# Scale and offset of the first expert layer: from its output to its activation

## The chip, the core and the metric

One core of a Trainium2 chip runs the whole program. The metric is the device time of one execution in microseconds; a run's time is the median over its executions. The tensor engine (TensorE, PE in the profile) multiplies; VectorE (DVE), ScalarE (ACT) and GpSimd (POOL) work element by element; SyncE (SP) issues transfers. PEld is TensorE's loading of the stationary operand, which runs beside its products.

## The reference

Three layers follow each other, all in float32. The first is a linear attention over 4 batches, 8 heads, 576 positions and 64 features a head: queries and keys pass through a softmax (the keys over the positions, with their maximum over the positions subtracted first), keys times values give a 64 by 64 matrix for each head, and queries times that matrix give 2304 tokens of 512 features. Two layers of 2048 hidden units follow.

```
h = x @ w_in
r = max(h, 0)
g = s * (r * r) + b          # s and b are one number each
x = g @ w_out                # first layer
h = x @ w_in2
g = h * tanh(softplus(h))
out = g @ w_out2             # second layer
```

The weights come as 64-bit floats, which the kernel turns into float32 on chip.

## The kernel before

**Steps.** The tokens are cut into five chunks of 512, 256, 512, 512 and 512. A step is one chunk with one block of 128 of the 2048 hidden units: 16 steps a chunk, 80 for the first layer (`ph` 0), then 80 for the second (`ph` 1). In a step `emit_h` makes h of a block from x, the activation makes g, and `emit_y` adds g times the block of `w_out` into the chunk's y, which stays in PSUM for 16 steps and is copied out by `y_out`. h is made two steps (`LEAD`) ahead of the y that uses it, in the second layer three.

**High and low halves.** Most products are made in three passes over a rounded high half and a low half: `split` lets ScalarE copy a tile to its high half (L171) and VectorE subtract it for the low half (L168, `minus`); `passes` issues three matmuls (L178). A step has 24 of them, 12 for h and 12 for y. The first steps of chunk 0 use whole float32 weights instead (L231, L284).

**The first layer's activation.** `emit_relu2` lets ScalarE take Relu out of PSUM (L258) and Square in place (L259), then splits. So g lacks s and b. `y_out` multiplies by s as it copies y out of PSUM (L313 on VectorE, L319 on ScalarE). The offset b reaches y as b times the column sums of `w_out`: `colsum` lets GpSimd add up the 32 blocks of `w_out`, high and low (L554, L556), into `acc`; `colsum_mm` sums over the partitions with eight narrow matmuls (L562) and multiplies by b (L566) into `bsum`; `x_split` adds `bsum` where the second layer takes its input (L202, L203).

**Attention.** A chunk's attention runs during the chunk before it, for two heads at a time (`hp` 0 to 3), in stages `att1` to `att5` one or two steps apart. Where a chunk reaches into a new batch, the keys are loaded into one buffer `kb` (L346, L350), and `att1` finds their maxima: a reduction on VectorE (L405), a transpose on TensorE (L410), a second reduction (L411), a product with the identity (L412), and a product with a tile of ones that spreads the maxima over all partitions (L413). `att2` subtracts them from the keys (L428), and with that frees `kb`. For the queries, L418 and L419 subtract maxima, L441 to L443 form reciprocal sums, L451 scales. L496 to L502 finish the 64 by 64 matrices, L471, L480 and L178 with `x` are TensorE's part.

**Weights.** `conv_bits` and `conv_split` turn 64-bit weights into float32 halves, five instructions on VectorE and a split for each of 16 pieces a layer; the first layer's in the first 140 us, the second layer's from the last chunk of the first layer on.

**Order.** `todo` and `run` put the stages at steps. That fixes the order in which the program is written; a planner with costs of its own then orders the instructions of each engine and sets buffers and semaphores. Each engine runs its list strictly in order, and SyncE its transfers, each of which waits for its buffer.

Of the kernel before, what the change touches and what calls it, by code (L numbers as in the profile page):

```python
# [26 lines left out]
def kernel(  # L27
# [47 lines left out]
    sb_s = const.tile([P, 1], F32, name="sb_s")  # L75
    sb_b = const.tile([P, 1], F32, name="sb_b")
    ones = const.tile([P, P], F32, name="ones")
    bsum = const.tile([P, NK], F32, name="bsum")
    y_dram = [dram.tile([P, NK, CHUNKS[c]], F32, name=f"yd{c}") for c in range(NC)]


# [88 lines left out]
    def split(hi, lo, src, eng=None):  # L170
        nc.scalar.copy(out=hi, in_=src)  # L171
        minus(eng or nc.vector, lo, src, hi)
# [21 lines left out]
    def x_split(ph, c, kk):  # L194
        n = CHUNKS[c]
        src = x_next.pop((ph, c, kk))
        hi, lo = (t[:, 0:n] for t in x_tiles(kk, f"{ph}_{c}_{kk}"))
        if ph == 0:
            split(hi, lo, src)
        else:  # L200
            b = bsum[:, kk:kk + 1]
            nc.scalar.activation(out=hi, in_=src, func=AF.Identity, bias=b)  # L202
            nc.vector.scalar_tensor_tensor(  # L203
                out=lo, in0=src, scalar=b, in1=hi.bitcast(F32), op0=ALU.add, op1=ALU.subtract
            )
        x_t[ph, c, kk] = (hi, lo)

    def x2_load(c):
# [40 lines left out]
    def emit_relu2(m):  # L249

        c = steps[m][1]
        if whole_y(m):
            r = gp.tile([P, CM], F32, tag="gl", name=f"r{m}")[:, 0:CHUNKS[c]]
            g_t[m] = (None, r)
        else:
            r = rp.tile([P, CM], F32, tag="r", name=f"r{m}")[:, 0:CHUNKS[c]]
            hi, lo = g_tiles(m)
        nc.scalar.activation(out=r, in_=h_ps.pop(m), func=AF.Relu)  # L258
        nc.scalar.activation(out=r, in_=r, func=AF.Square)  # L259
        if not whole_y(m):  # L260
            split(hi, lo, r)

    def emit_mish(m):

# [27 lines left out]
    def y_out(n):  # L292
        ph, c, _ = steps[n]
        nt = CHUNKS[c]
        nm = NK if ph == 0 else nt // P
        w = nt if ph == 0 else DM
        if ph == 0:
            to = y_dram[c]
        else:
            to = out[T0[c]:T0[c] + nt, :].rearrange("(p r) d -> p r d", p=P)  # L300
        for m, ps in enumerate(y_ps.pop((ph, c))):
            if m % 2 == 0:
                pair = cv.tile([P, 2 * DM], F32, tag="t", name=f"ys{m}_{n}")
                pair = pair.rearrange("p (i d) -> p i d", i=2)
            ys = pair[:, m % 2, 0:w]
            if n == 2 * NS - 1 and m == nm - 1:
                nc.sync.dma_start(out=to[:, m - 1, :], in_=pair[:, 0, 0:w])
                for copy, o in ((nc.scalar.copy, slice(0, w // 2)), (nc.vector.tensor_copy, slice(w // 2, w))):
                    copy(out=ys[:, o], in_=ps[:, o])
                    nc.sync.dma_start(out=to[:, m, o], in_=ys[:, o])  # L310
                continue
            if m % 2 and ph == 0:
                nc.vector.tensor_scalar(  # L313
                    out=ys, in0=ps[:, 0:w], scalar1=sb_s, scalar2=None, op0=ALU.mult
                )
            elif m % 2:
                nc.vector.tensor_copy(out=ys, in_=ps[:, 0:w])
            elif ph == 0:
                nc.scalar.activation(out=ys, in_=ps[:, 0:w], func=AF.Copy, scale=sb_s)  # L319
            else:  # L320
                nc.scalar.copy(out=ys, in_=ps[:, 0:w])
            if m % 2:
                nc.sync.dma_start(out=to[:, m - 1:m + 1, :], in_=pair[:, :, 0:w])
# [66 lines left out]
    def att1(b, c, hp):  # L390

        if b is not None:
            kb = kv_in[b, hp][0]
            if b == 0:
                ke = q_raw[hp][:, 2 * DM:4 * DM]
                km = ke[:, RK * P:(RK + 1) * P]
                kc = ke[:, (RK + 1) * P:(RK + 1) * P + 1]
                ke = ke[:, 0:RK * P].rearrange("p (r h d) -> p r h d", r=RK, h=2)
            else:
                ke = ap.tile([P, RK, 2, D], F32, tag="ke", name=f"ke{b}_{hp}")  # L400
                km = ap.tile([P, P], F32, tag="km", name=f"km{b}_{hp}")
                kc = ap.tile([P, 1], F32, tag="kc", name=f"kc{b}_{hp}")


            nc.vector.tensor_reduce(  # L405
                out=km.rearrange("p (h d o) -> p h d o", h=2, o=1),
                in_=kb.rearrange("p h r d -> p h d r"), axis=AX.X, op=ALU.max,
            )
            ps = att_ps(b == 0, hp % 2, f"km{b}_{hp}")
            nc.tensor.transpose(ps[:, 0:P], km, ident)  # L410
            nc.vector.tensor_reduce(out=kc, in_=ps[:, 0:P], axis=AX.X, op=ALU.max)  # L411
            nc.vector.tensor_scalar(out=km, in0=ident, scalar1=kc, scalar2=None, op0=ALU.mult)  # L412
            nc.tensor.matmul(out=ps[:, P:2 * P], lhsT=ones, rhs=km, start=True, stop=True)  # L413
            kv_mid[b, hp] = (ps[:, P:2 * P].rearrange("p (h d) -> p h d", h=2), ke)
        rq = CHUNKS[c] // P
        t = q_in[c, hp].rearrange("p h r d -> p (h r) d")
        mx = ap.tile([P, 2 * CM // P, 1], F32, tag="qm", name=f"qm{c}_{hp}")[:, 0:2 * rq, :]
        nc.vector.tensor_reduce(out=mx, in_=t, axis=AX.X, op=ALU.max)  # L418
        (nc.vector if c else nc.gpsimd).tensor_tensor(  # L419
            out=t, in0=t, in1=mx.to_broadcast([P, 2 * rq, D]), op=ALU.subtract  # L420
        )

    def att2(b, c, hp):
        if b is not None:
            kb = kv_in[b, hp][0]
            km, ke = kv_mid[b, hp]
            for h in range(2):
                nc.vector.tensor_tensor(  # L428
                    out=ke[:, :, h, :], in0=kb[:, h], in1=km[:, h:h + 1, :].to_broadcast([P, RK, D]),
                    op=ALU.subtract,  # L430
                )
        nc.scalar.activation(out=q_in[c, hp], in_=q_in[c, hp], func=AF.Exp)

    def att3(b, c, hp):
        if b is not None:
            ke = kv_mid[b, hp][1]
            nc.scalar.activation(out=ke, in_=ke, func=AF.Exp)
        rq = CHUNKS[c] // P
        t = q_in[c, hp].rearrange("p h r d -> p (h r) d")
# [22 lines left out]
    def att4_mm(b, c, hp):  # L462

        if b is not None:
            vb = kv_in.pop((b, hp))[1]
            ke = kv_mid.pop((b, hp))[1]
            ps = att_ps(b == 0, hp % 2, f"kv{b}_{hp}")
            kv_ps[b, hp] = ps
            for r in range(RK):
                for h in range(2):  # L470
                    nc.tensor.matmul(  # L471
                        out=ps[h * D:(h + 1) * D, 0:D + 1], lhsT=ke[:, r, h],
                        rhs=vb[:, r, h * (D + 1):(h + 1) * (D + 1)],
                        start=(r == 0), stop=(r == RK - 1),
                    )
# [67 lines left out]
        x_next[0, c, hp] = t  # L543


    acc = []

    def colsum(f):
        if f == 0:
            acc.append(wp.tile([P, 4 * DM], F32, tag=f"w{WHOLE - 1}", name="acc")[:, 0:DM])  # L550
        for i, w in enumerate(W[0, "wo", f]):
            w = w.bitcast(F32)
            if f == 0 and i == 0:
                op = nc.gpsimd.tensor_copy(out=acc[0], in_=w)  # L554
            else:
                op = nc.gpsimd.tensor_tensor(out=acc[0], in0=acc[0], in1=w, op=ALU.add)  # L556
            tc.keep_in_program_order(op)

    def colsum_mm():
        ps = ps_a.tile([P, CM], F32, tag="a", name="bsum_ps")  # L560
        for kk in range(NK):
            nc.tensor.matmul(  # L562
                out=ps[:, kk:kk + 1], lhsT=acc[0][:, kk * P:(kk + 1) * P], rhs=ones[:, 0:1],
                start=True, stop=True,
            )
        nc.vector.tensor_scalar(  # L566
            out=bsum, in0=ps[:, 0:NK], scalar1=sb_b, scalar2=None, op0=ALU.mult
        )


    todo = {}

    def at(slot, what, fn, *args):
# [29 lines left out]
            at(s + o[4], "att5_mm", att5_mm, b, c, hp)  # L603
    for i, c in enumerate(ORDER2):
        at((NC - 1 + i) * NF, "load", x2_load, c)
    for f in range(NF):
        at(2 * NF + 12 + f, "sum", colsum, f)
    at(3 * NF + 12, "sum", colsum_mm)

# [18 lines left out]
    for hp in range(NP):  # L630
# [4 lines left out]
        if hp:  # L635
            v_load(0, hp - 1)
    v_load(0, NP - 1)
    run(-3, "load")
    bds.append(ap.tile([P, P], F32, name="bd"))
    nc.vector.memset(bds[NP], 0.0)  # L640
    v_pads(vb1)
    nc.gpsimd.memset(kb1[REST:P, :, RK - 1, :], -3.0e38)
    nc.sync.dma_start(out=sb_s, in_=moe_s[0:1].partition_broadcast(P))
    nc.sync.dma_start(out=sb_b, in_=moe_b[0:1].partition_broadcast(P))
    run(-2, "load")
    for hp in range(NP):
        for stage in (att1, att2, att3, att4_mm, att4, att5, att5_mm):
# [8 lines left out]
    for n in range(2 * NS):  # L656
# [12 lines left out]
        for m in hs:  # L669
# [6 lines left out]
                emit_relu2(m)  # L676
                continue
            emit_mish(m)
        run(n, "att5_mm", "att4", "att1", "sum")
        if not boundary and n < 2 * NS - 2:  # L680
            emit_y(n)
        elif n == 2 * NS - 2:
# [43 lines left out]
```

## Time and profile before

| | |
|---|---|
| median of 3 runs | 896.02 us (896.01 to 896.61) |
| profiled execution, its own time | 897.58 us |
| its span, first to last instruction | 895.8 us |
| TensorE busy | 861.5 us, 96% |
| VectorE / ScalarE / GpSimd busy | 415.2 / 349.6 / 54.4 us |
| mean granted TensorE clock | 0.988 |

All views are of the one profiled execution. Its time is longer than its span by what lies before the first and behind the last instruction. An engine that is busy all the time need not be at its peak: the granted clock says at which of its two levels, 1.2 or 2.4 GHz, TensorE ran. In the timeline, square brackets hold the idle time in front of an instruction and what ended it.

### The profile page before, as it was taken

Reading aid. Unit: us, or ns where it says so; the run is one execution under the profiler, and the core shown is the slowest. Engines: PE = TensorE matmul, PEld = TensorE weight load, DVE = VectorE, ACT = ScalarE, POOL = GpSimd, SP = SyncE. Lnnn points to the kernel's source line nnn. Section 1 sums busy time; section 2 is a strip of 40 time slices with the busy share of each in tenths; the row PEclk is TensorE's granted clock in tenths of the full one; section 3 lists DMA queues with packets and bytes.
Section 4 is the critical chain, followed back from the end, with each engine's and each line's share of the span. In section 5 each row is a group of like instructions: output and inputs, shape, how many; then the busy total and the mean of one; then the engine's idle time right before and its main releaser. Section 6 shows DMA issues by size and latency. Waiting matters only on the chain.

```text
span 895.8 us, 10587 instructions
## 1 busy us (share of the span) xinstructions
PE 861.5 (96%) x4220; PEld 698.8 (78%) x4220; DVE 415.2 (46%) x667; ACT 349.6 (39%) x627; POOL 54.4 (6%) x65
## 2 busy tenths in 40 slices
PE   4799997879999999999999999999999999999997
PEld 3344786879888888888888888888889888888886
DVE  6989988866354422225883488311112211121111
ACT  3645674435554543444545233321122321132211
POOL 4000006920000000000000000000000000000000
PEclk9999997989999999999999999999999999999999
DMA  8992114122111010022542152010011100001001
GB/s 226 314 369 66 33 30 120 27 56 59 50 42 47 12 48 12 1 83 105 188 142 78 63 182 101 25 48 0 1 48 48 45 27 1 0 1 48 1 0 48
DMA packets 59490, 62.56 MB, mean 70 GB/s; under 512 B 24240, under 2 KB 51120, under 8 KB 59440
## 3 DMA queue, kind: packets, MB, share of 16 engines
q1 hardware_dynamic: 58352, 60.83, 21.2%
q10 hardware_dynamic: 1088, 1.05, 0.4%
q8 instruction: 33, 0.54, 0.3%
q14 instruction: 17, 0.14, 0.0%
HBM read 52.43 MB, written 9.44 MB: 69 GB/s over the span
## 4 chain that ended last, share of the span: by engine, by line
PE 91%; DVE 4%; DMA 2%; SPq 1%; issue 1%; ACT 0%; POOL 0%; DVEq 0%
PE y L178 41%; PE h L178 40%; PE h L231 4%; PE y L284 3%; DMA kb<-in_k_dram 2%; PE x L178 1%; PE kv L471 1%; PE qt L480 1%; DVE qn L451 1%; DVE gl L168 1%; DMA kvb<-in_k_dram 1%; PE km L413 0%; DVE km L412 0%; DMA q<-in_q_dram 0%; DVE qs L442 0%
## 5 line engine op out<-in xcount | busy, mean ns | idle before, releaser
L178 PE MATMUL h<-xh,w 128*128 128x512 f32 (+1 forms) x1208 | 367.3, 371 | 0.0
L168 DVE TENSOR_TENSOR gl<-r,gh 128x512 fp32r<-128x512 f32 (+1 forms) x152 | 100.7, 664 | 343.5 <-ACT r L269 259.2
L178 PEld LDWEIGHTS h<-xh,w 128*128 128x128 f32 x1208 | 223.7, 191 | 38.3 <-ACT r L258 0.3
L178 PE MATMUL h<-xl,w 128*128 128x512 f32 (+1 forms) x604 | 223.4, 370 | 0.7 <-DVE xl L168 0.7
L178 PE MATMUL y<-gh,w 128*128 128x512 f32 (+1 forms) x584 | 178.3, 370 | 0.0
L178 PE MATMUL y<-w,gh 128*128 128x512 f32 x568 | 175.1, 390 | 0.0
L268 ACT ACTIVATE gh<-h 128x512 fp32r<-128x512 f32 (+1 forms) x79 | 43.8, 555 | 242.0 <-PE y L178 216.8
L178 PEld LDWEIGHTS h<-xl,w 128*128 128x128 f32 x604 | 115.5, 191 | 19.9 <-DVE xl L168 0.9
L178 PEld LDWEIGHTS y<-w,gh 128*128 128x128 f32 x568 | 105.6, 188 | 21.1
L178 PEld LDWEIGHTS y<-gh,w 128*128 128x128 f32 x584 | 107.7, 190 | 17.7
L178 PE MATMUL y<-gl,w 128*128 128x512 f32 (+1 forms) x292 | 108.4, 372 | 2.9 <-DVE gl L168 2.8
L178 PE MATMUL y<-w,gl 128*128 128x512 f32 x284 | 110.3, 389 | 0.0
L258 ACT ACTIVATE r<-h 128x512 f32<-128x512 f32 (+1 forms) x80 | 44.1, 554 | 111.9 <-PE h L178 103.5
L178 PEld LDWEIGHTS y<-gl,w 128*128 128x128 f32 x292 | 55.6, 190 | 12.2 <-DVE gl L168 3.4
L178 PEld LDWEIGHTS y<-w,gl 128*128 128x128 f32 x284 | 53.3, 188 | 11.2
L171 ACT CAST w<-t 128x1024 fp32r<-128x1024 f32 x32 | 33.5, 1051 | 53.6 <-DVE t L154 50.1
L259 ACT ACTIVATE r<-r 128x512 f32<-128x512 f32 (+1 forms) x80 | 46.8, 589 | 1.8
L269 ACT ACTIVATE r<-h 128x512 f32<-128x512 f32 (+1 forms) x80 | 44.0, 551 | 0.0
L171 ACT CAST gh<-r 128x512 fp32r<-128x512 f32 (+1 forms) x73 | 41.7, 574 | 3.2 <-PE y L178 1.5
L556 POOL TENSOR_TENSOR acc<-acc,w 128x512 f32<-128x512 f32 x31 | 41.8, 1349 | 2.4
L168 DVE TENSOR_TENSOR w<-t,w 128x1024 fp32r<-128x1024 f32 x32 | 39.0, 1220 | 4.0 <-ACT w L171 3.9
L150 DVE SCALAR_TENSOR_TENSOR t<-raw,t 128x1024 int32<-128x1024 int32 x32 | 39.0, 1222 | 0.2
(102 smaller groups left out, 605.3 us busy)
## 6 DMA issues: line engine op xcount, KB each, us to landing
raw<-in_moe_w_in_dram SPq DMA_DIRECT2D x32, 512.0 KB, 5.3
raw<-in_moe_w_out_dram SPq DMA_DIRECT2D x32, 512.0 KB, 6.8
yd<-ys SPq DMA_DIRECT2D x8, 512.0 KB, 2.6
x<-yd SPq DMA_DIRECT2D x16, 256.0 KB, 3.8
out_dram<-ys SPq DMA_DIRECT2D x8, 512.0 KB, 2.7
kb<-in_k_dram SPq DMA_DIRECT2D x12, 256.0 KB, 2.9
vb<-in_v_dram SPq DMA_DIRECT2D x24, 128.0 KB, 3.0
kvb<-in_k_dram SPq DMA_DIRECT2D x4, 256.0 KB, 3.7
```

What stands on the lines that cost most here:

```text
L150: nc.vector.scalar_tensor_tensor(out=ti, in0=high, scalar=-0x40000000, in1=ti, op0=ALU.bitwise_and, op1=ALU.bitwise_or,)
L168: eng.tensor_tensor(out=lo, in0=src, in1=hi.bitcast(F32), op=ALU.subtract)
L171: nc.scalar.copy(out=hi, in_=src)
L178: mm = nc.tensor.matmul(out=ps, lhsT=x, rhs=y, start=start, stop=stop)
L231: nc.tensor.matmul(out=h_ps[m], lhsT=wl[:, o], rhs=x_whole[kk], start=kk == 0, stop=kk == NK - 1,)
L258: nc.scalar.activation(out=r, in_=h_ps.pop(m), func=AF.Relu)
L259: nc.scalar.activation(out=r, in_=r, func=AF.Square)
L268: nc.scalar.activation(out=hi, in_=h_ps[m], func=AF.Mish)
L269: nc.scalar.activation(out=r, in_=h_ps.pop(m), func=AF.Mish)
L284: nc.tensor.matmul(out=ps[:, 0:nt], lhsT=wl[:, o], rhs=gl, start=f == 0, stop=False)
L451: (nc.vector if c else nc.gpsimd).tensor_tensor(out=qn[:, :, h, :], in0=t[:, o, :], in1=sm[:, o, :].to_broadcast([P, rq, D]), op=ALU.mult)
L556: op = nc.gpsimd.tensor_tensor(out=acc[0], in0=acc[0], in1=w, op=ALU.add)
```

## The change

g is made as the reference has it. In chunks 0 and 1 ScalarE applies s and b after Square with one more instruction. In chunks 2 to 4 VectorE makes s r r from r, ScalarE adds b as it makes the high half, and VectorE adds b and subtracts the high half for the low one. `colsum`, `colsum_mm`, `acc` and `bsum` go; `y_out` copies without s, and `x_split` splits the second layer's input as it does the first's. s and b are loaded ahead of the first weights. Besides, the product that spreads the key maxima (L413) moves from the end of `att1` to the head of `att2`, one step later.

```
-    bsum = const.tile([P, NK], F32, name="bsum")
...
-        if ph == 0:
-            split(hi, lo, src)
-        else:
-            b = bsum[:, kk:kk + 1]
-            nc.scalar.activation(out=hi, in_=src, func=AF.Identity, bias=b)
-            nc.vector.scalar_tensor_tensor(
-                out=lo, in0=src, scalar=b, in1=hi.bitcast(F32), op0=ALU.add, op1=ALU.subtract
-            )
+        split(hi, lo, src)
...
         nc.scalar.activation(out=r, in_=h_ps.pop(m), func=AF.Relu)
-        nc.scalar.activation(out=r, in_=r, func=AF.Square)
-        if not whole_y(m):
-            split(hi, lo, r)
+        if c < 2:
+            nc.scalar.activation(out=r, in_=r, func=AF.Square)
+            nc.scalar.activation(out=r, in_=r, func=AF.Identity, scale=sb_s, bias=sb_b)
+            if not whole_y(m):
+                split(hi, lo, r)
+            return
+        nc.vector.scalar_tensor_tensor(
+            out=r, in0=r, scalar=sb_s, in1=r, op0=ALU.mult, op1=ALU.mult
+        )
+        nc.scalar.activation(out=hi, in_=r, func=AF.Identity, bias=sb_b)
+        nc.vector.scalar_tensor_tensor(
+            out=lo, in0=r, scalar=sb_b, in1=hi.bitcast(F32), op0=ALU.add, op1=ALU.subtract
+        )
...
-            if m % 2 and ph == 0:
-                nc.vector.tensor_scalar(
-                    out=ys, in0=ps[:, 0:w], scalar1=sb_s, scalar2=None, op0=ALU.mult
-                )
-            elif m % 2:
+            if m % 2:
                 nc.vector.tensor_copy(out=ys, in_=ps[:, 0:w])
-            elif ph == 0:
-                nc.scalar.activation(out=ys, in_=ps[:, 0:w], func=AF.Copy, scale=sb_s)
             else:
                 nc.scalar.copy(out=ys, in_=ps[:, 0:w])
...
             nc.vector.tensor_scalar(out=km, in0=ident, scalar1=kc, scalar2=None, op0=ALU.mult)
-            nc.tensor.matmul(out=ps[:, P:2 * P], lhsT=ones, rhs=km, start=True, stop=True)
-            kv_mid[b, hp] = (ps[:, P:2 * P].rearrange("p (h d) -> p h d", h=2), ke)
+            kv_mid[b, hp] = (ps[:, P:2 * P], km, ke)
...
     def att2(b, c, hp):
         if b is not None:
             kb = kv_in[b, hp][0]
-            km, ke = kv_mid[b, hp]
+            ps, km, ke = kv_mid[b, hp]
+            nc.tensor.matmul(out=ps, lhsT=ones, rhs=km, start=True, stop=True)
+            km = ps.rearrange("p (h d) -> p h d", h=2)
...
-    acc = []
-
-    def colsum(f):
...
-    def colsum_mm():
...
-    for f in range(NF):
-        at(2 * NF + 12 + f, "sum", colsum, f)
-    at(3 * NF + 12, "sum", colsum_mm)
...
     v_load(0, NP - 1)
+    nc.sync.dma_start(out=sb_s, in_=moe_s[0:1].partition_broadcast(P))
+    nc.sync.dma_start(out=sb_b, in_=moe_b[0:1].partition_broadcast(P))
     run(-3, "load")
...
-    nc.sync.dma_start(out=sb_s, in_=moe_s[0:1].partition_broadcast(P))
-    nc.sync.dma_start(out=sb_b, in_=moe_b[0:1].partition_broadcast(P))
     run(-2, "load")
```

## Rows read from the trace of the kernel before

**Rows 1.** The page's 40 equal slices: busy share in tenths, TensorE and GpSimd.

```profile
PE   4799997879999999999999999999999999999997
...
POOL 4000006920000000000000000000000000000000
```

**Rows 2.** Windows, 143 to 191.6 us: stretch, length, busy (instructions) by engine, granted clock, DMA.

```profile
core 0: us, PE busy (x) PEld busy (x) DVE busy (x) ACT busy (x) POOL busy (x), PEclk, DMA share, GB/s
142.97:151.22 8.25, 2.84 (x17) 1.99 (x16) 7.61 (x14) 2.19 (x7) 7.78 (x7) 0.77 0.61 179
151.22:157.60 6.38, 6.33 (x28) 6.04 (x29) 3.71 (x7) 3.01 (x8) 6.07 (x5) 0.50 0.25 83
157.60:181.18 23.58, 20.71 (x191) 19.54 (x190) 20.62 (x24) 9.95 (x25) 22.25 (x18) 1.00 0.10 27
...
185.73:191.60 5.87, 5.87 (x27) 5.87 (x28) 2.18 (x8) 3.35 (x8) 0.00 (x0) 0.50 0.18 50
```

**Rows 3.** TensorE's timeline, its three longest gaps behind 45 us.

```profile
151.22 0.80 PE L413 MATMUL km<-km,ones 128*128 128x128 f32 x2 [3.72 <-DVE km L412]
...
161.76 0.39 PE L178 MATMUL y<-gl,w 128*128 128x256 f32 x1 [1.96 <-DVE gl L168]
...
185.73 0.80 PE L413 MATMUL km<-km,ones 128*128 128x128 f32 x2 [4.55 <-DVE km L412]
```

**Rows 4.** GpSimd's timeline, 128 to 200 us.

```profile
141.41 44.19 POOL L556 TENSOR_TENSOR acc<-acc,w 128x512 f32<-128x512 f32 x31
```

**Rows 5.** VectorE's groups by form, 140.7 to 185.6 us: count, busy us, mean ns, idle before.

```profile
L168 DVE TENSOR_TENSOR gl<-r,gh 128x256 fp32r<-128x256 f32 x8 | 7.8, 1000 | 0.0
L451 DVE TENSOR_TENSOR qn<-q,qs 128x256 f32<-128x256 f32 x4 | 5.7, 1452 | 0.0
L412 DVE TENSOR_SCALAR km<-ident,kc 128x128 f32<-128x128 f32 x3 | 3.8, 1257 | 0.0
L442 DVE TENSOR_SCALAR qs<-qs 128x8 f32<-128x8 f32 x3 | 3.7, 1239 | 0.0
...
L405 DVE TENSOR_REDUCE km<-kb 128x128 f32<-128x640 f32 x2 | 2.6, 1324 | 4.4 <-DMA kb<-in_k_dram 4.4
```

**Rows 6.** VectorE's groups by form, 190 to 260 us.

```profile
L405 DVE TENSOR_REDUCE km<-kb 128x128 f32<-128x640 f32 x4 | 5.2, 1312 | 2.5 <-DMA kb<-in_k_dram 2.5
...
L451 DVE TENSOR_TENSOR qn<-q,qs 128x256 f32<-128x256 f32 x8 | 3.0, 422 | 5.3 <-PE x L178 5.3
L168 DVE TENSOR_TENSOR gl<-r,gh 128x256 fp32r<-128x256 f32 x7 | 2.9, 415 | 3.3 <-ACT gh L171 3.3
...
L412 DVE TENSOR_SCALAR km<-ident,kc 128x128 f32<-128x128 f32 x3 | 0.9, 286 | 0.1
...
L442 DVE TENSOR_SCALAR qs<-qs 128x8 f32<-128x8 f32 x4 | 0.7, 167 | 0.0
```

**Rows 7.** Windows, 84 to 140 us.

```profile
84.00:140.00 56.00, 56.00 (x282) 43.63 (x281) 50.05 (x83) 39.37 (x64) 0.00 (x0) 1.00 0.15 39
```

**Rows 8.** ScalarE's groups by form from 190, VectorE's from 260, to 860 us.

```profile
L259 ACT ACTIVATE r<-r 128x512 f32<-128x512 f32 x48 | 30.3, 632 | 1.1
...
L202 ACT ACTIVATE xh<-x,bsum 128x512 fp32r<-128x512 f32 x16 | 10.8, 722 | 1.5 <-PE h L178 1.5
...
L203 DVE SCALAR_TENSOR_TENSOR xl<-x,bsum,xh 128x512 fp32r<-128x512 f32 x16 | 11.1, 749 | 2.1 <-ACT xh L202 2.1
```

**Rows 9.** TensorE's timeline at 396 us.

```profile
396.01 0.95 PE L562 MATMUL bsum_ps<-ones,acc 128*128 128x1 f32 x8
```

**Rows 10.** Windows, two stretches of chunk 4.

```profile
419.68:430.56 10.88, 10.88 (x50) 9.01 (x49) 9.98 (x13) 5.33 (x8) 0.00 (x0) 1.00 0.31 103
474.08:484.96 10.88, 10.88 (x50) 9.01 (x49) 1.70 (x3) 3.93 (x8) 0.00 (x0) 1.00 0.16 65
```

**Rows 11.** Timelines of SyncE's queue and of ScalarE at the start.

```profile
19.77 0.43 SPq L643 DMA_DIRECT2D sb_s<-in_moe_s_dram  x1
...
23.94 1.15 ACT L142 ACTIVATE t<-raw 128x1024 f32<-128x1024 f32 x1
```

**Rows 12.** The chain that ended last, at 153 us: start, us, what.

```profile
153.40 3.80 DMA kb<-in_k_dram
```

More of the change, by code (lines that the diff above doesn't have):

```diff
@@ L435, in att3 @@
         if b is not None:
-            ke = kv_mid[b, hp][1]
+            ke = kv_mid[b, hp][2]
             nc.scalar.activation(out=ke, in_=ke, func=AF.Exp)
@@ L465, in att4_mm @@
             vb = kv_in.pop((b, hp))[1]
-            ke = kv_mid.pop((b, hp))[1]
+            ke = kv_mid.pop((b, hp))[2]
             ps = att_ps(b == 0, hp % 2, f"kv{b}_{hp}")
@@ L543, in att5_mm @@
         x_next[0, c, hp] = t
-    acc = []
-    def colsum(f):
[L549 to L557, printed above, removed]
-    def colsum_mm():
[L560 to L568, printed above, removed]
     todo = {}
@@ L678 @@
             emit_mish(m)
-        run(n, "att5_mm", "att4", "att1", "sum")
+        run(n, "att5_mm", "att4", "att1")
         if not boundary and n < 2 * NS - 2:
```

## The prediction

> **What bounds the kernel now.** I began with the page's forty slices [rows 1]. TensorE stands at 9 tenths nearly everywhere, so only its gaps can be won, and they lie in two places: the first two slices, and slices 7 to 9, where it reads 7, 8 and 7. GpSimd's row reads 6, 9 and 2 in exactly those three slices and nothing after. A slice is 895.8 / 40 = 22.4 us, so the place is 134 to 201 us: the end of chunk 0 and most of chunk 1, the narrow one.
>
> Next I cut this place at the gaps with the view of windows [rows 2]. TensorE's idle time is length less busy time: 8.25 - 2.84 = 5.41 us, 6.38 - 6.33 = 0.05 and 23.58 - 20.71 = 2.87; between the third row's end and the fourth's begin lies one more gap, the 4.55 us of [rows 3]. Together 12.88 us. Two rows, 6.38 and 5.87 us long, show a granted clock of 0.50, which is 1.2 instead of 2.4 GHz, each right behind a gap of about 4 us. Before the third, 1.96 us gap of [rows 3] the clock was 1.00, and in its window it stayed 1.00.
>
> Then TensorE's timeline says what ended the gaps [rows 3]: both long ones end at L413, the product that spreads the key maxima, waiting for VectorE's L412; the third waits for the low half of g. All three are VectorE's lateness. Why it is late shows in its own groups by form, once inside GpSimd's stretch [rows 5] and once behind it [rows 6]; GpSimd's stretch is one row, 31 additions in 44.19 us [rows 4], 1.4 us each. Same line, same shape, two prices: the low half of g 1000 against 415 ns, L451 1452 against 422, L442 1239 against 167 although it touches only 8 columns, L412 1257 against 286. The control is L405, a reduction with one input: 1324 against 1312. So some VectorE instructions sit out a GpSimd addition and others don't. The four groups lose 8 x 0.585 + 4 x 1.030 + 3 x 1.072 + 3 x 0.971 = 14.9 us, more than TensorE's whole idle time here.
>
> This is what the Trainium skill's page "SBUF — State Buffer", section "Who interferes with whom", states: VectorE and GpSimd share one pair of ports, taken for a whole instruction, by VectorE instructions with two inputs in SBUF or in a two-port mode, and never by a reduction. The groups agree (1239 against 167, 1324 against 1312); a reader who trusts the rows alone gets the same sum.
>
> **The change, part by part.**
>
> *GpSimd's column sums go.* VectorE gets its 14.9 us back, and the gaps that its lateness made should close. How far? In the first window (5.41 us idle) the delayed work ahead of TensorE is one L442, one pair of L451 and one L412: 1.07 + 2.06 + 0.97 = 4.10 us, which leaves 1.31. That is plausible, since there TensorE needs the last part of x for chunk 1 and has little else to do. Bounds: 0 to 5.41; I take 1.31. Ahead of the 4.55 us gap are one each of L442 and L412, a pair of L451 and a low half: 1.07 + 0.97 + 2.06 + 0.59 = 4.69, so nothing is left. For the 2.87 us between them, the 1.96 of [rows 3] among them, 14.9 - 4.10 - 4.69 = 6.1 us of lateness are left; I take 0. Idle time won: 12.88 - 1.31 = **11.6 us** (bounds 4.6, if 5.41 and 2.87 stay, and 12.9).
>
> *The clock.* With gaps of at most 1.3 us the clock should stay up, as it did around the 1.96 us gap. Work of 6.33 and 5.87 us at half the clock [rows 2] then takes half: 3.17 + 2.94 = **6.1 us** won. Bounds: 0, if a gap like the 3.72 us one stays, to 6.1.
>
> *The eight small products of the sums* [rows 9] sit among dense TensorE work: **0.95 us** won (0 at least).
>
> *The product moved to the next step.* It issues no DMA, and the count stays. In [rows 3] it is where TensorE stood twice; a step later, L412 has the y products' time to finish, so the move is a second cover for the same gaps, not a second gain. What it costs: the subtraction from the keys (L428) follows it, the reload of the single key buffer follows that, and on VectorE the row sums of the step queue behind the subtraction. The spreading itself is 0.8 us of TensorE on either side of the move. Where the kernel had no gap I take 0, for TensorE has y and h products on both sides to run; the price without that cover is the first rival's.
>
> *g = s r^2 + b in chunks 0 and 1* adds one ScalarE instruction a step. The trace of before has none with scale and bias from a tile in this place; the nearest are Square at 632 ns and the biased copy L202 at 722 [rows 8]. Sixteen in chunk 0 are 10.1 to 11.6 us, off TensorE's path as long as ScalarE keeps up. From 84 to 140 us, the fullest part, it is busy 39.37 of 56.00 us [rows 7]; about ten steps fall into it, 7.2 us, and 9.4 stay free. TensorE is busy all 56.00 us there, and h runs two steps ahead of y. One step is 24 products, 5.2 us by the 50 in 10.88 us of [rows 10], so 0.7 us more of latency is covered: 0. Without cover it would be 11.6 us.
>
> *In chunks 2 to 4* (48 steps) ScalarE loses its Square and VectorE gains a product of 749 ns by L203's form [rows 8]; the chain to g now passes from ScalarE to VectorE and back twice. The fullest row of VectorE is 9.98 of 10.88 us at 420 us, while second-phase weights are converted [rows 10]. Two more instructions make 11.48: over by 0.6. But the conversions are what fills it and they can slip: at 474 us VectorE is busy 1.70 of 10.88. Taken: 0; the price if not is the last rival's.
>
> *Evictions and second-phase input* only lose an operand. *Loads of s and b* move ahead of the first weight loads on SyncE's queue, which then start 2 x 0.43 = 0.86 us later [rows 11]. ScalarE's first use of weights, at 23.94 us, begins right behind its previous instruction, so part of this is hidden; VectorE is the bound of that stretch. Bounds 0 and 0.86; I take **+0.3**.
>
> **Sum** against the profiled execution: 897.58 - 11.6 - 6.1 - 0.95 + 0.3 = 879.2. The median of the runs is 896.02, 1.56 below that execution, so 877.7.
>
> **The rivals.**
>
> *The key loads take the gaps over.* There is one key buffer; its reload needs the subtraction, and the subtraction now waits for the later product. The chain shows one such load at 3.80 us [rows 12], and VectorE stood 4.4 us for two inside GpSimd's stretch [rows 5]. For it: behind that stretch VectorE still waits 2.5 us for four [rows 6]. Against it: TensorE is not held there. If two loads come to lie on the path, 7.6 us return, and with one gap long enough a half-clock stretch of 3.2: 885 to 888.5.
>
> *The lateness isn't GpSimd's.* Then only the small products go: 897.58 - 0.95 + 0.3 - 1.56 = 895.4, no measurable change. Against it stands the split between two-input work and reductions.
>
> *Slower: the longer chain to g starves y in chunks 2 to 4.* If VectorE's queue, over-full at 420 us, makes TensorE wait at each of the 48 steps, the gain of 18.3 us is eaten at 0.38 us a step; at 0.5 it is 24 us and 902. For it: 11.48 us of work for 10.88. Against it: h leads by two steps, 10 us, against some 3 us of chain, and the fullness is work that can be put off.
>
> **How the numbers follow.** My forecast has a chance of 0.62, the key loads 0.22, the unrelated lateness 0.06, the starved y 0.06, and 0.04 is for mixtures that keep some of the gain. All won, the floor is 897.58 - 12.9 - 6.1 - 0.95 - 1.56 = 876.1. The forecast's own range is 875.8 to 882; the upper end of mine, 887.5, takes in two thirds of the key-load case and leaves 0.19 out. A measurement of this kernel tells some 0.2%, 1.8 us, from no change. Faster by more: 0.62 + 0.22 + 0.04 = 0.88; within: 0.06, the second rival; slower: 0.06, the third.
>
> **What would show it.** Right: GpSimd empty after 30 us; L442 near 170 and L451 near 420 ns in chunk 1; no wait above 2 us at L413; the granted clock at 1.00 from 140 to 200 us; TensorE dense from 45 us to the tail but for a gap of about 1.3 us at the start of chunk 1. Wrong: a TensorE wait for keys or q (first rival), the old prices of L442 without GpSimd (second), or waits of y for the low half of g in chunks 2 to 4 (third). My weakest step is the 1.31 us left over at the chunk's start: the instruction order is planned anew, and work that I count as hidden may land on that path.

## The result, and the profile after

The changed kernel takes **881.5 us** (median of 4 runs, 880.89 to 881.83) beside 896.01 (4 runs, 895.22 to 896.61): the ratio is 0.9838, 95% interval [0.9821, 0.9855]. Run again in a later group it took 883.36 (5 runs, 881.35 to 884.3) beside 896.47, ratio 0.9851 [0.9836, 0.9866]. The forecast of 877.7 lies below all these runs; its range holds them.

Page slices of the changed kernel, TensorE, GpSimd and granted clock, to be laid beside [rows 1]:

```profile
PE   4799998999999999999999999999999999999997
...
POOL 4000000000000000000000000000000000000000
PEclk9999999999999999999999999999999999999999
```

GpSimd is empty behind the first slice, and where TensorE read 7, 8, 7 it reads 8, 9, 9. The reason is in VectorE's groups by form, 139 to 205 us, which answer to [rows 5] (the names of lines have moved: L439 was L442, L448 was L451, L408 was L412, L401 was L405, and, for later, L406 was L410, L425 was L428 and L422 is the moved L413):

```profile
L167 DVE TENSOR_TENSOR gl<-r,gh 128x256 fp32r<-128x256 f32 x16 | 6.7, 421 | 5.5 <-ACT gh L170 5.5
L401 DVE TENSOR_REDUCE km<-kb 128x128 f32<-128x640 f32 x4 | 5.2, 1298 | 5.1 <-DMA kb<-in_k_dram 5.1
L448 DVE TENSOR_TENSOR qn<-q,qs 128x256 f32<-128x256 f32 x10 | 3.8, 421 | 3.0 <-PE x L177 2.9
...
L408 DVE TENSOR_SCALAR km<-ident,kc 128x128 f32<-128x128 f32 x5 | 1.4, 277 | 0.0
L439 DVE TENSOR_SCALAR qs<-qs 128x8 f32<-128x8 f32 x6 | 1.0, 165 | 0.0
```

The four disturbed groups fell to the prices of [rows 6]; the one-input reduction L401 stayed at 1298 ns. What TensorE still waits for, from 44 us to the tail (wait, total us, times, longest):

```profile
PE km L406 <- DVE km L401: 1.3, 1, 1.3
PE km L422 <- DVE km L408: 0.8, 1, 0.8
PE h L177 <- DVE xl L167: 0.3, 1, 0.3
PE h L177 <- ACT r L250: 0.2, 1, 0.2
```

All four lie between 140 and 155 us. The two long waits for the spreading product [rows 3] are gone, but a new one heads the list: the key transpose L406, waiting for the key maximum L401. And between the end of chunk 0 and the tail the clock still falls once (windows of 1 us in the changed kernel):

```profile
145.00:146.00 1.00, 0.48 (x4) 0.48 (x4) 0.89 (x3) 0.50 (x2) 0.00 (x0) 1.00 1.01 210
146.00:147.00 1.00, 0.78 (x7) 0.58 (x5) 0.88 (x2) 0.41 (x2) 0.00 (x0) 0.99 0.78 228
147.00:148.00 1.00, 0.98 (x4) 0.98 (x5) 0.42 (x1) 1.00 (x3) 0.00 (x0) 0.50 0.63 211
...
149.00:150.00 1.00, 1.00 (x7) 1.00 (x7) 0.69 (x1) 0.97 (x2) 0.00 (x0) 0.50 0.35 96
150.00:151.00 1.00, 1.00 (x9) 1.00 (x8) 0.00 (x0) 1.00 (x4) 0.00 (x0) 0.80 0.06 13
```

From 147 to 150 us TensorE is busy at a granted clock of 0.50, that is 1.2 GHz.

**One table for all traces.** Every trace is cut at two points of TensorE's timeline: the end of chunk 0's last y product, and the first y product of chunk 2. Between them, *idle* is length less busy time, and *clock* is busy time times (1 less granted clock), summed over windows of 1 us. *Rest* is what remains of the span, dense work in the main. Microseconds:

| kernel | chunk 0 ends | idle | clock | rest | span |
|---|---|---|---|---|---|
| before | 141.60 | 12.87 | 6.31 | 735.02 | 895.8 |
| changed | 140.56 | 2.65 | 1.64 | 734.25 | 879.1 |
| changed, later group (e12) | 141.54 | 3.82 | 1.69 | 734.25 | 881.3 |
| e1, no sums | 141.57 | 3.78 | 1.69 | 733.66 | 880.7 |
| e2, move only | 141.46 | 11.49 | 6.38 | 734.57 | 893.9 |
| e3, not moved | 141.58 | 2.58 | 1.63 | 734.51 | 880.3 |
| e4, sums back | 140.52 | 12.19 | 6.31 | 734.98 | 894.0 |
| e5, sums late | 141.63 | 3.82 | 1.56 | 735.59 | 882.6 |
| e6, loads back | 140.54 | 4.72 | 3.39 | 734.35 | 883.0 |
| e7, no reload | 140.84 | 1.33 | 0.00 | 735.23 | 877.4 |
| e8, pair earlier | 142.55 | 3.34 | 0.00 | 734.91 | 880.8 |
| e9, all VectorE | 140.86 | 6.87 | 4.39 | 735.48 | 887.6 |
| e10, all ScalarE | 141.99 | 2.84 | 1.65 | 734.22 | 880.7 |
| e11, pair later | 141.01 | 4.28 | 1.70 | 736.31 | 883.3 |

The rest stays within 1.4 us of before's; nearly the whole effect is idle and clock time in this one place. For the changed kernel the terms against before are -1.04, -10.22, -4.67 and -0.77, together -16.7; in the later group -0.06, -9.05, -4.62 and -0.77, together -14.5. These are differences of single traced executions; by medians the changed kernel is 14.5 us faster in the first group (896.01 - 881.5) and 13.1 in the later one (896.47 - 883.36).

### The profile page after: what moved, and what is told of

It is laid out like the page before. It is cut to its first block, busy times and chain, and to the rows that moved or that the text cites. A ratio compares the mean times of both kernels' runs of the same rounds, so it can differ in the third digit from the quotient of the medians.

```text
span 879.1 us, 10563 instructions
## 1 busy us (share of the span) xinstructions
PE 854.4 (97%) x4212; PEld 693.2 (79%) x4212; DVE 431.0 (49%) x714; ACT 344.2 (39%) x611; POOL 12.4 (1%) x33
## 4 chain that ended last, share of the span: by engine, by line
PE 95%; DVE 2%; DMA 1%; ACT 1%; issue 0%; POOL 0%; SPq 0%; DVEq 0%; ACTq 0%
PE y L177 43%; PE h L177 42%; PE h L223 4%; PE y L286 3%; PE x L177 1%; PE kv L468 1%; PE qt L477 1%; DMA kvb<-in_k_dram 1%; DMA kb<-in_k_dram 0%; PE km L422 0%; DVE q L401 0%; PE x L525 0%; DVE xl L167 0%; PE km L406 0%; DVE qs L438 0%
## 5 line engine op out<-in xcount | busy, mean ns | idle before, releaser
L167 DVE TENSOR_TENSOR gl<-r,gh 128x512 fp32r<-128x512 f32 (+1 forms) x104 | 63.1, 608 | 265.3 <-ACT r L271 259.6
L177 PE MATMUL y<-gl,w 128*128 128x512 f32 (+1 forms) x292 | 106.6, 367 | 0.0
L257 DVE SCALAR_TENSOR_TENSOR r<-r,sb_s 128x512 f32<-128x512 f32 x48 | 35.9, 748 | 56.4 <-ACT r L250 56.3
L260 ACT ACTIVATE gh<-r,sb_b 128x512 fp32r<-128x512 f32 x48 | 34.8, 724 | 37.6 <-DVE r L257 34.9
L261 DVE SCALAR_TENSOR_TENSOR gl<-r,sb_b,gh 128x512 fp32r<-128x512 f32 x48 | 35.9, 749 | 21.0 <-ACT gh L260 20.8
```

What stands on the lines that cost most here:

```text
L167: eng.tensor_tensor(out=lo, in0=src, in1=hi.bitcast(F32), op=ALU.subtract)
L177: mm = nc.tensor.matmul(out=ps, lhsT=x, rhs=y, start=start, stop=stop)
L257: nc.vector.scalar_tensor_tensor(out=r, in0=r, scalar=sb_s, in1=r, op0=ALU.mult, op1=ALU.mult)
L260: nc.scalar.activation(out=hi, in_=r, func=AF.Identity, bias=sb_b)
L261: nc.vector.scalar_tensor_tensor(out=lo, in0=r, scalar=sb_b, in1=hi.bitcast(F32), op0=ALU.add, op1=ALU.subtract)
```

## The experiments

The theory is that of the prediction: GpSimd's additions hold up VectorE in chunk 1, TensorE waits for VectorE, its clock falls. The rivals are the moved product (that the gain comes from the move), the key load, and the new forms of g.

| run | median us (range, runs) | before, same group | ratio, 95% interval |
|---|---|---|---|
| e1 | 882.17 (881.45 to 883.95, 4) | 895.93 | 0.985 [0.9829, 0.9871] |
| e2 | 895.09 (893.91 to 896.53, 10) | 895.93 | 0.9995 [0.9983, 1.0006] |
| e3 | 882.94 (882.07 to 884.51, 4) | 895.93 | 0.9861 [0.9837, 0.9885] |
| e4 | 896.1 (894.23 to 896.92, 10) | 895.93 | 1.0003 [0.9993, 1.0013] |
| e5 | 884.62 (882.0 to 885.15, 4) | 895.86 | 0.9873 [0.9854, 0.9892] |
| e6 | 885.27 (882.62 to 886.19, 4) | 895.86 | 0.9881 [0.9861, 0.9902] |
| e7 | 880.01 (879.13 to 880.46, 4) | 895.86 | 0.9829 [0.9812, 0.9845] |
| e8 | 882.1 (880.39 to 882.62, 4) | 895.86 | 0.9847 [0.9831, 0.9863] |
| e9 | 889.64 (889.38 to 891.83, 4) | 896.47 | 0.9928 [0.9914, 0.9942] |
| e10 | 882.61 (881.92 to 883.1, 4) | 896.47 | 0.9843 [0.983, 0.9857] |
| e11 | 885.24 (884.09 to 886.54, 4) | 896.47 | 0.9874 [0.986, 0.9887] |
| e12 | 883.36 (881.35 to 884.3, 5) | 896.47 | 0.9851 [0.9836, 0.9866] |

**e1: before, without the column sums** (and so without b).

```
-    for f in range(NF):
-        at(2 * NF + 12 + f, "sum", colsum, f)
-    at(3 * NF + 12, "sum", colsum_mm)
...
+    nc.vector.memset(bsum, 0.0)
```

Expected: 

> The kernel before without the column sums on GpSimd and without their eight small products; the offset that they carry is set to zero, so b is left out of the result. Nothing else is changed. If VectorE's lateness from 141 to 186 us is GpSimd's doing, L442 falls from 1239 to about 170 ns and L451 from 1452 to about 420 there, and the time falls by most of what the change won: 881 to 885 us. If the moved product or the new form of g made the gain, the old prices stay and the time is 894 to 896 us.

Measured: 882.17 us, about the whole gain with one part of the change. VectorE's prices fell as expected: L442 to 166 and L451 to 421 ns from 139 to 205 us.

**e2: before, with the spreading product moved, alone.**

```
-            nc.tensor.matmul(out=ps[:, P:2 * P], lhsT=ones, rhs=km, start=True, stop=True)
...
     def att2(b, c, hp):
...
+            nc.tensor.matmul(out=ps, lhsT=ones, rhs=km, start=True, stop=True)
```

Expected: 

> The kernel before with the spreading product alone moved from the end of att1 to the head of att2. If the gaps are VectorE's lateness, the product only meets it elsewhere: L442 stays near 1240 ns, and 892 to 897 us come out. If TensorE's place in the order was the cause, the two gaps of 3.72 and 4.55 us go, with the half-clock stretches behind them, and the time is 881 to 885 us.

Measured: 895.09, no change. VectorE's prices stand as in [rows 5] and the product waits a step later, for the same instruction (groups by form of e2, 139 to 190 us, and its first wait of TensorE; L452 and L443 were L451 and L442, and L426 is the moved product):

```profile
L452 DVE TENSOR_TENSOR qn<-q,qs 128x256 f32<-128x256 f32 x4 | 4.5, 1168 | 0.2 <-PE x L178 0.2
...
L412 DVE TENSOR_SCALAR km<-ident,kc 128x128 f32<-128x128 f32 x3 | 3.8, 1251 | 0.0
L443 DVE TENSOR_SCALAR qs<-qs 128x8 f32<-128x8 f32 x3 | 3.7, 1243 | 0.0
```

```profile
PE km L426 <- DVE km L412: 6.4, 2, 3.5
```

**e3: the changed kernel, with the product back in its old place.** The edit is e2's, the other way round.

Expected: 

> The changed kernel with the spreading product back at the end of att1; sums gone and g made the new way. If the sums are the cause, the product's place is worth within 2 us either way: 880 to 884 us. If the place is the cause, 893 to 896 us. It also shows whether the start, which became 1.1 us shorter with the change, owes that to the product's place (the first y would begin near 45.4 us again) or not (44.3).

Measured: 882.94, with idle 2.58 and clock 1.63 as in the changed kernel. The move is worth nothing in either direction.

**e4: the changed kernel, with GpSimd's additions back** at their old step; nothing uses their result.

```
...
+    for f in range(NF):
+        at(2 * NF + 12 + f, "sum", colsum, f)
...
-        run(n, "att5_mm", "att4", "att1")
+        run(n, "att5_mm", "att4", "att1", "sum")
```

Expected: 

> The changed kernel with GpSimd's 32 column-sum instructions put back, their result used by nobody, and without the eight small products. g is made the new way and the spreading product is in its new place. If GpSimd's additions slow VectorE, L439 goes from 165 back to about 1240 ns in chunk 1 and most of the gain is lost: 890 to 896 us, unless the later place of the product now covers a part of the lateness (then 885 to 890). If they are not the cause, 881 to 882 us.

Measured: 896.1: all of the gain is lost, idle 12.19 and clock 6.31 stand about as before. VectorE's prices are up again, if not all to the old height (139 to 190 us: L439 976 ns, L448 1384, L408 911). With e1 this settles the cause: additions that feed nothing cost some 14 us.

**e5: before, with the additions held back to chunk 2.** They wait for one column of the g of chunk 2's thirteenth step.

```
             if f == 0 and i == 0:
+                late = nc.gpsimd.tensor_copy(out=acc[0][:, 0:1], in_=g_t[2 * NF + 12][0][:, 0:1].bitcast(F32))
+                tc.keep_in_program_order(late)
```

Expected: 

> The kernel before, with its GpSimd column sums held back: GpSimd first copies one column of a late step's g into the accumulator, so that its 31 additions of 1.4 us begin only in chunk 2 (behind about 250 us) and not at 141 us. Everything else, the place of the spreading product too, stays as before. If it is the place of the additions in the narrow chunk 1 that costs the time, the two long gaps and the half-clock stretches of chunk 1 go as they did without the sums, and the additions delay VectorE in a stretch where it has room: 881 to 885 us. If the additions cost the same wherever they lie (44 us in which VectorE's two-input instructions are held up), the gaps appear in chunk 2: 892 to 897. If the time went by leaving out b and the small products and not by GpSimd, 895.

Measured: 884.62, the full work of before and 11.2 us less. Idle 3.82 and clock 1.56 in the stretch of the table stand as in e1. The additions now run from 280.7 to 327.3 us, over the end of chunk 2 and the start of chunk 3 (GpSimd's group in e5):

```profile
L558 POOL TENSOR_TENSOR acc<-acc,w 128x512 f32<-128x512 f32 x31 | 44.2, 1427 | 2.4
```

VectorE's groups by form from 280 to 328 us, in e5:

```profile
L168 DVE TENSOR_TENSOR gl<-r,gh 128x512 fp32r<-128x512 f32 x8 | 10.3, 1283 | 13.9 <-ACT gh L171 13.9
...
L451 DVE TENSOR_TENSOR qn<-q,qs 128x256 f32<-128x256 f32 x2 | 2.0, 1054 | 3.6 <-PE x L178 3.6
...
L419 DVE TENSOR_TENSOR q<-q,qm 128x512 f32<-128x512 f32 x1 | 1.2, 1248 | 0.0
...
L418 DVE TENSOR_REDUCE qm<-q 128x8 f32<-128x512 f32 x1 | 0.7, 686 | 1.0 <-DMA q<-in_q_dram 1.0
```

The same lines from 280 to 328 us of before, where no addition runs:

```profile
L168 DVE TENSOR_TENSOR gl<-r,gh 128x512 fp32r<-128x512 f32 x8 | 5.5, 690 | 15.1 <-ACT gh L171 15.1
...
L451 DVE TENSOR_TENSOR qn<-q,qs 128x256 f32<-128x256 f32 x4 | 1.5, 423 | 6.8 <-PE x L178 6.8
...
L419 DVE TENSOR_TENSOR q<-q,qm 128x512 f32<-128x512 f32 x2 | 1.4, 692 | 0.1
L418 DVE TENSOR_REDUCE qm<-q 128x8 f32<-128x512 f32 x2 | 1.4, 690 | 1.6 <-DMA q<-in_q_dram 1.6
```

VectorE is held up there too (1283 against 690 ns, 1054 against 423, 1248 against 692; the reduction L418 is not, 686 against 690). But it has idle time in front of its work, and TensorE waits there once:

```profile
PE h L178 <- DVE xl L168: 0.4, 1, 0.4
```

The Trainium skill's page "SBUF — State Buffer", section "Who interferes with whom", gives the lock on the shared ports and who takes it; these prices agree. What the lock costs the kernel is another matter: some 14 us in chunk 1; in the later place 0.4 us of waiting in the trace, and at most some 2.5 us by medians of two groups (884.62 less e1's 882.17, small products included).

**e6: the changed kernel, with the loads of s and b in their old place.**

```
-    nc.sync.dma_start(out=sb_s, in_=moe_s[0:1].partition_broadcast(P))
-    nc.sync.dma_start(out=sb_b, in_=moe_b[0:1].partition_broadcast(P))
     run(-3, "load")
...
+    nc.sync.dma_start(out=sb_s, in_=moe_s[0:1].partition_broadcast(P))
+    nc.sync.dma_start(out=sb_b, in_=moe_b[0:1].partition_broadcast(P))
     run(-2, "load")
```

Expected: 

> The changed kernel with the loads of s and b in their old place, behind the first weight loads. If the loads ahead of the weights cost start time, as predicted (0.3 us, at most 0.86), this is 0.3 to 0.9 us faster than the changed kernel, near 880.9, and the first dense y product stands before 44.3 us. If they are what brought the start forward by 1.1 us (44.3 against 45.4), it is 1.1 us slower, near 882.6, with the first y at 45.4. If they do neither, 881.5 and 44.3.

Measured: 885.27, slower than every case expected, but not at the start: the first y product stands at 44.13 us in e6 and at 44.15 in the changed kernel, and chunk 0 ends at 140.54 and 140.56. The whole 3.9 us between the spans lies in the stretch of the table (idle +2.07, clock +1.75). TensorE's timeline of e6 there:

```profile
149.84 0.28 PE L177 MATMUL h<-xh,w 128*128 128x256 f32 x1
153.50 0.44 PE L406 MATMUL km<-ident,km 128*128 128x128 f32 x1 [3.37 <-DVE km L401]
```

The same wait as in the changed kernel, 3.37 instead of 1.32 us. e12, unaltered, shows 2.49: so this wait varies between runs of one kernel, and e6 doesn't tell what the loads' order is worth. The traces do show where the wait of e6 comes from: the key load took 4.66 us in e6 and 3.76 in e12, 0.90 more for 0.88 more of wait. (In the changed kernel's first trace it took 4.09; there the h products, slowed by the half clock, filled part of the time.)

**e7: the changed kernel, without one reload of the key buffer**; batch 2's second head pair reads the keys of its first.

```
     def kv_load(b, hp):
...
+        if (b, hp) == (2, 1):
+            return
```

Expected: 

> The changed kernel without one reload of the key buffer: batch 2's second head pair uses the keys of the first (the output of that batch's attention differs). It is the reload that lands at 151.5 us and that the key maximum waits for. If this load sets the gap of 1.32 us ahead of the key transpose at 153 us and the lateness of the low half of g behind it, the gap goes, the half-clock stretch at 147 to 151 us stays or shrinks, and the time is 879 to 880.5 us. If the load is only near the path and the thin work at the chunk's start sets the time, 881.5 us and the same gap with another name on it.

Measured: 880.01. In the traced execution the wait at the key transpose is gone, and the half clock, expected to stay or shrink, is gone with it. TensorE's waits, 44 to 860 us (L424 and L410 were L422 and L408):

```profile
PE km L424 <- DVE km L410: 0.8, 1, 0.8
PE h L177 <- DVE xl L167: 0.3, 1, 0.3
PE h L177 <- ACT r L250: 0.2, 1, 0.2
```

Idle 1.33 and clock 0.00 are what the prediction wrote for the change itself (1.31 and 0). The load in e12, in the chain that ended last (start, us, what):

```profile
147.03 0.90 DVE ke L425 x2
...
147.94 0.39 SPq L342
...
148.37 3.76 DMA kb<-in_k_dram
...
152.23 1.25 DVE km L401
...
153.62 0.30 PE km L406
```

The subtraction L425 frees the single key buffer, the load follows, then the maximum, then the transpose: 6.6 us from the subtraction's start to the transpose, while TensorE ran out of h products at 151.1 (153.62 less its wait of 2.49).

**e8: the changed kernel, chunk 2's first head pair one step earlier.**

```
-            s = (c - 1) * NF + 3 * hp - 1 if c > 1 else 2 * hp + 3
+            s = (c - 1) * NF + 3 * hp - 1 - ((c, hp) == (2, 0)) if c > 1 else 2 * hp + 3
```

Expected: 

> The changed kernel with the attention of chunk 2's first head pair planned one step earlier, so that its key work, and the reload behind it, lie further ahead of chunk 1's start. If what is left at the boundary (about 2.65 us idle and 4 us at half the clock) is this attention work bunching there, it shrinks by 1 to 4 us: 877.5 to 880.5 us. If it is the lack of other TensorE work at the boundary, 881.5; if the earlier step only pulls the waits into the end of chunk 0, 882 to 885.

Measured: 882.1, no gain. TensorE no longer waits at L406 but for the low half of g, which stands in VectorE's order behind the key maximum and its wait for the load (TensorE's timeline of e8):

```profile
156.36 0.39 PE L177 MATMUL y<-gl,w 128*128 128x256 f32 x1 [2.00 <-DVE gl L167]
```

**e11: the changed kernel, chunk 2's second head pair one step later** (the same line, with `+ ((c, hp) == (2, 1))`). The next pair's keys are then loaded ahead of this pair's subtraction, which works on them: the output of that pair differs.

Expected: 

> The changed kernel with the attention of chunk 2's second head pair planned one step later. Its key transpose then stands behind the first y products of chunk 1 in TensorE's order, and not ahead of them, and the key load that it waits for has some 5 us more. If that load is what is left at the boundary (2.3 us between the changed kernel and the one without the reload), the 1.3 to 3.4 us wait ahead of the key transpose goes and the time is 879 to 880.5 us. If a wait for something else takes its place, 881 to 882; if the later step pushes the pair's work into the next one, 883 or more.

Measured: 885.24. The wait went where e8's went (1.9 us for the low half of g), and some h products came late by small waits; idle is 4.28. A later transpose doesn't help while VectorE's queue holds the maximum ahead of g.

**e9: the changed kernel, g by VectorE's form in chunks 0 and 1 too,** but for the first steps of chunk 0, which use whole weights.

```
-        if c < 2:
+        if whole_y(m):
```

Expected: 

> The changed kernel with the VectorE form of g in chunks 0 and 1 too, except in the steps that aren't split: one product of some 750 ns a step moves from ScalarE to VectorE. VectorE is busy 50.8 of 56.0 us from 84 to 140 us; some ten steps of that make 58, over by 2. If VectorE's load in chunk 0 is on the path, TensorE waits there and the time is 883 to 886 us; if there is slack behind it, 881.5.

Measured: 889.64 beside e12's 883.36 in the same group. Not in the body of chunk 0, where TensorE stays dense, but at its end: VectorE comes out of it late (windows of e9, then its first wait of TensorE):

```profile
84.00:140.00 56.00, 56.00 (x281) 43.65 (x280) 52.54 (x87) 34.85 (x54) 0.00 (x0) 1.00 0.15 39
...
146.00:156.00 10.00, 8.58 (x37) 7.46 (x37) 7.80 (x21) 5.26 (x14) 0.00 (x0) 0.52 0.45 113
```

```profile
PE x L177 <- DVE qtl L167: 4.4, 3, 2.5
```

**e10: the changed kernel, g by ScalarE's form everywhere** (`if c < NC:`).

Expected: 

> The changed kernel with the ScalarE form of g in chunks 2 to 4 too: one product a step moves from VectorE to ScalarE there. The prediction took either chain as covered at nothing, since h runs two steps ahead of y: 881.5 us, within 1. If the longer chain or the extra ScalarE work is on the path at any of the 48 steps, TensorE shows waits of y for g and the time is above 884; if VectorE's part of the chain cost something, it is below 880.

Measured: 882.61, the same as e12. From 300 to 500 us ScalarE is busy 110.90 instead of 69.28 us, VectorE 91.45 instead of 114.21, and TensorE 200.00 of 200.00 in both (e10, then e12):

```profile
300.00:500.00 200.00, 200.00 (x890) 165.47 (x889) 91.45 (x125) 110.90 (x169) 0.00 (x0) 1.00 0.23 81
```

```profile
300.00:500.00 200.00, 200.00 (x891) 165.46 (x890) 114.21 (x157) 69.28 (x104) 0.00 (x0) 1.00 0.23 81
```

**e12: the changed kernel, unaltered, once more.**

Expected: 

> The changed kernel, unaltered, beside the others of this group: 881.5 us. If its runs spread to 885 us, the 3.8 us between it and the kernel with the loads of s and b in their old place is the spread of the stretch at the start of chunk 1, and not those loads; if they stay within 880.5 to 882.5, the order of the loads matters there.

Measured: 883.36, 881.35 to 884.3; with the first four runs, one kernel spans 880.89 to 884.3.

## Why the prediction was right, and where its sizes were off

*The cause* was right: the column sums gone give the gain (e1), put back they take it (e4), and the move is worth 0 (e2, e3), as the sum had it. The reason given for that, "a second cover for the same gaps", doesn't hold: alone the move covers little, 6.4 of the 8.3 us that TensorE waited for the product in before stay in e2.

*The weakest step failed where it said it might:* "which leaves 1.31". Idle time left is 2.65 and 3.82 us in the two traces of the changed kernel; 1.33 is left only without the reload of e7. What the working had put down to VectorE's lateness alone has a second thing behind it, the key load, which the lateness had hidden. So the idle term is 10.2 and 9.1 us instead of 11.6.

*The clock* was the other: "With gaps of at most 1.3 us the clock should stay up". It came back by 4.7 and 4.6 of the 6.1 us. In the first trace the clock fell behind no gap over 0.84 us, in e12 behind the wait for the keys. What the step rested on, half clock "each right behind a gap of about 4 us", was read too coarsely: [rows 2] has 0.77 in the window that ends with the first long gap. Finer windows of before show the fall:

```profile
146.60:147.60 1.00, 0.89 (x4) 0.48 (x3) 0.89 (x3) 0.15 (x2) 0.92 (x2) 0.91 0.89 225
147.60:148.60 1.00, 0.00 (x0) 0.00 (x0) 1.00 (x2) 0.70 (x2) 0.92 (x2) 0.50 0.69 167
```

A mean of 0.91 leaves 0.18 us at 0.50, so the clock fell at 147.42 us, and the gap of 3.72 us began at 147.50. So the first fall of before was not the long gap's doing, and a fall at the same place, 147.0 us, stands in the changed kernel. Without the reload the clock stayed up in the traced execution (mean of its whole span 0.999); e7's other three show 0.995 to 0.997, so whether it stayed up in them isn't shown. One execution of e12 has a mean of 1.000 and is with 881.35 us the shortest of its five: one and the same kernel runs with the fall and without it.

*The first rival* held in part: its mechanism is there, at one load instead of two. By the table the changed kernel has 4.29 - 1.33 = 3.0 us more than e7 in the first trace and 4.2 in e12, idle and clock together, not the 7.6 and 3.2 that the rival set. Of this the wait itself is 1.3 and 2.5 us; in the first trace the clock fell ahead of the wait, so whether the load has a part in that 1.64 isn't shown. By medians the difference is less clear, 880.01 beside 881.5 and 883.36 in other groups.

*From the terms to the forecast.* The result lies 881.5 - 877.7 = 3.8 us above the forecast. For the traced execution it is 1.7 (880.89 beside the sum's 879.2): idle and clock time won are 1.4 us short each, and chunk 0 ended 1.04 us sooner where the sum had +0.3. The other 2.2 us are the step to medians: the sum took off 1.56 us because before's traced execution lay that far above its median, and the changed kernel's lay 0.6 below its own. e7's span of 877.4 meets the sum's 895.8 - 18.3 = 877.5, with idle and clock time as forecast. That start and rest, -0.76 and +0.21, add up to about the sum's +0.3 and -0.95 is luck, and e7's median is 2.3 us above the forecast.

*The other terms.* Small products 0.95: the rest fell by 0.77 in both traces, but over all kernels without these products it lies between 733.66 and 736.31, with them between 734.57 and 735.59, so no run shows this term. Loads of s and b +0.3: not to be seen; the changed kernel's first y stands at 44.15 us in one execution and at 45.15 in the other, and a price of this size can't be told from that spread. The new g at 0: right in chunks 2 to 4 (e10 agrees, and TensorE never waits for g there, which ends the third rival), and right in chunk 0 because the square goes on ScalarE; on VectorE it costs 6.3 us (e9), so it matters which engine has the room. The second rival fell with e1 and with L439 at 165 ns.

*What stays open:* why the key load took 4.66 us in e6 and 3.76 in e12, and whether the order of the loads has a part in it; why the clock falls in one execution and not in another; and whether a second key buffer would win e7's time, which no run shows. No run that does the whole computation was faster than the changed kernel beyond its spread.

## What to carry to other kernels

Look at the same instruction inside and outside another engine's stretch, and split by kind: two-input work and tensor_scalar slowed on VectorE while reductions did not, and that pointed to GpSimd before any run; e1 and e4 then showed it. An off-path engine's work need not be removed, only put where the engine that it holds up has room (e5 won 11.2 us of some 14 by that). And when a stall is taken away, price the next thing in the same queue, here a load behind a single buffer, as a part of the forecast and not only as a rival; moving the instruction that waits (e8, e11) only moves the wait to what stands behind it.

## What the runs showed of the hardware that was not expected

The clock doesn't follow the longest gap alone. It fell to 0.50 in the changed kernel with no gap over 0.84 us in front, TensorE busy 0.69, 0.48 and 0.78 of three successive microseconds. In e12, the same kernel, TensorE was busy 0.66, 0.50 and 0.76 in the same place, and the clock stayed at 1.00 there; in e8, after gaps of the same sizes and then one of 2.00 us, it stayed at 1.00 from the end of chunk 0 to the tail. In e12 a wait of 2.49 us was followed by about 3.4 us at half, in e6 one of 3.37 us by about 6.8 (twice the table's clock terms). A half clock ahead of the key wait went with less time lost than one behind it: idle and clock together 4.29, 4.21 and 4.49 us in the changed kernel, e3 and e10, where it fell ahead, and 5.51, 5.47 and 5.38 in e12, e1 and e5, where it fell behind. The likely reason is that the slow h products filled part of the time until the keys came (the wait was 1.32 us in the changed kernel); no run tests it.

The start is not fixed: the first y product of chunk 0 stands between 44.13 us (e6) and 46.12 us (e8), although TensorE's groups of products up to there come in the same order in e8 as in the changed kernel. A difference of 1 us between two profiled spans need not be the change's.
